# A re-searched instruction order for two transformer layers on one core, with another x tile on ScalarE and an earlier start of the first weight sums

## The chip, the cores and the metric

The kernel runs on one core of a Trainium2 chip. The metric is device microseconds of one execution, the median of three runs. The core has TensorE (PE, the matrix multiplier, with weight loads shown apart as PEld), VectorE (DVE), ScalarE (ACT), GpSimd (POOL) and SyncE (SP), which here issues nearly all DMA transfers. Each engine takes its instructions strictly in the order in which the program lists them, and they wait for each other by semaphores.

## What is computed

Two layers, each made of an attention block A and a feed-forward block B, over x of 2048 rows and 1024 columns:

```python
x = x + A(layernorm(x), wqkv, wo)
x = x + B(layernorm(x), w1, b1, w2, b2)   # and the same pair once more
# A: q, k, v = x @ wqkv; each of 32 heads looks at 8 rows back in steps of 2;
#    softmax over the 8; weighted sum of v; @ wo
# B: h = relu(x @ w1 + b1)**2; h @ w2 + b2      (3584 hidden columns)
```

## The kernel before

The rows are cut into four blocks of 512 rows, and the two layers make eight units (unit 0 to 7), each a block in a layer. A block is four tiles of 128 rows. A unit runs through these stages, named by the functions that write them:

- `SA` loads the four x tiles and normalises them into `xnA`, with features on the partitions. For unit 0 the tiles are loaded in the order 0, 1, 3, 2 (`ORD`). Three of them go through `ln_first`: mean and variance by DVE (`bn_stats`, L791, and their aggregation, L793), the reciprocal root by ACT (L784, L785), the normalisation by DVE (L788). The tile that `LNA` names goes through `ln` instead: ACT makes its statistics by two passes over the tile (L746, L750) with small steps between (L747, L753, L754); if the tile is in `LNV`, DVE normalises it (L759), else ACT does (L756, L725). The normalised tiles of unit 0 are transposed on PE (L807) and copied out by DVE or ACT (L812).
- `SQ` multiplies `xnA` by the q, k and v weights (L888), and ACT writes the results out of PSUM (L893). In unit 0 the first sixteen chunks of k and q are made in halves: first for the tiles 0 and 1, later for 2 and 3. Later units use a seven-product form of block multiplication (`seven`, L663), which needs sums of weights and of inputs. The weight sums are made once and kept in DRAM: `keep_wqkv` (L531), `keep_w1` (L680), `keep_w2` (L457), `keep_wo` (L1108), each a chain of four DVE subtractions and additions with one store each (`sk`, `sqv`, `sw`, `tw`, `two`). The input sums are `TA` (L703) and `T` (L699), on DVE.
- `S2` is the attention: products of q and k on DVE (`P`, L950), their sums (L958), the sum over a head on PE (`lg`, L965), exp on ACT (L976), weighted v on DVE (L1029, L1036).
- `SW` or `SW7` multiplies by wo (L1084, L1155), `SF1` by w1 (L663 again, with L1323 and L1329 on ACT), `SF2` by w2 (L1388), with `yxa` and `yxo` (L1057, ACT) and `xm` (L1058, DVE) behind it.

No engine's order is written out by hand. `Plan` collects every operation with an engine, a planned duration, what it reads and writes, and a priority. `schedule` simulates the engines with these numbers and emits the operations in the order in which they started. `emit` does that several times: the lists in `ORDER` hold seeds, `shift` moves priorities at random by the seeds of the first list, and each later list takes the last schedule's start times as priorities and has `reshift` move some of them. So a list of seeds stands for a whole order of the program, and a change of any seed or of any dependency moves instructions on every engine.

What stands in the code where the change touches it: `ORDER` and the constants above it; in `SA` the branch `u == 0 and tl in LNA`, and the branch `tl == 1`, where `no` is the normalisation (L788) of the second tile; at the end of `SQ` the call of `keep_wqkv` for k in unit 0, whose last argument is a list of operations that the DVE sums (L531) have to follow:

```python
if u == 0 and tl in LNA:
    self.ln(x, xv, [0], xnT, tl, LNP, False, on_pe=True, tag="xn3", after=rst, vnorm=tl in LNV)
...
self.keep_wqkv(nm, ws[nm], [op for op in self.p.ops if op.name == "ptc"] if u == 0 else ())
```

Of the kernel before, what the change touches and what calls it, by code (L numbers as in the profile page):

```python
# [52 lines left out]
RAW = {1: (0, 0), 2: (0, 1), 4: (1, 1)}  # L53
COMB = (5, 7, 6, 3)
RT = 4
LNA = (2,)
LNP = -9e4
LNV = (3,)
AGF = True
FNO = True  # L60
CPA = (1,)
TAIL = True
CPT = ("xn3",)
PR1 = 20.0
# [3 lines left out]
GZ = 6  # L68

ORDER = [  # L70
    [254407839, 254101347, 254903199, 254319407, 254050087, 254927933, 254855223, 254245079, 254581483, 254651541, 254520156, 254414887, 254913701,
    254790479, 254811163, 254451245, 254423391, 254397903, 254011055, 254062271, 254611583, 254031453, 254777341, 254655655, 254059855, 254811767,
    254985755, 254068743, 254312045, 254255164, 254470565, 254340451, 254056147, 254532525, 254814045, 254382679, 254727165, 254873957, 254977849,
    254263075, 254189925, 254540757, 254064125, 254382964, 254486213, 254240707, 254389627, 254830877, 254011075, 254846617, 254426221, 254651009, ],
    [254887702, 254542295, 254553460, 254714252, 254435956, 254354174, 254720528, 254745279, 254184398, 254991686, 254429133, 254634373, 254093956,
    254465069, 254449012, 254670841, 254966233, 254766785, 254298535, 254990048, 254057679, 254666170, 254633564]]

MM = 0.2157
MMH = 0.1091
# [10 lines left out]
def act(n):  # L90
    return 0.05 + n * 0.00084
# [242 lines left out]
class _Kernel:  # L334
# [465 lines left out]
    def transpose(self, xn, xnT, tl, prio, parts=1, act=False):  # L800
# [3 lines left out]
        for i in range(parts):  # L804
# [3 lines left out]

            on_act = act or parts > 1 and i in CPA

# [16 lines left out]
    def SA(self, u):  # L827
        p = self.p
        layer, b = divmod(u, self.NB)
        st = self.state.setdefault(u, {})  # L830
        xnT = Buf("8K", "xnA1" if u == 1 else "xnA", [128, 4, self.KD, 128], F16)
        st["xnA"] = xnT
        after = [self.state[u - 2].get("gatef") or self.state[max(u - 2, 1)].get("gatev")] if u >= 2 else ()
        first, rst = (), []
        for tl in ORD if u == 0 else range(4):
            t = b * 4 + tl
            x, xv = self.load_x(layer, t, after, tag="x0" if u == 0 else "xt", prio=PR1 if u == 1 else -1e6 if u == 0 else None,
                                eng="ACT" if u == 0 and tl in XACT else "SP")
            if u == 0 and tl in LNA:
                self.ln(x, xv, [0], xnT, tl, LNP, False, on_pe=True, tag="xn3", after=rst, vnorm=tl in LNV)  # L840
            elif u == 0:
                bn, ag, r, rest = self.ln_first(x, xv, xnT, tl, first)
                rst.append(r)
                if tl == 0:
                    first, rest0 = [ag] if AGF else [bn], rest
                elif tl == 1:
                    rest0([ag])
                    c, xn, no = rest()
                    first = [no if FNO else c]
                    self.keep_clock(NPB, xn)  # L850
                else:
                    rest()
            else:
                self.ln(x, xv, [0], xnT, tl, PR1 if u == 1 else 20.0, False, vnorm=u in NORM)

    def SQ(self, u, jobs, order=None, halves=()):
        nc, p = self.nc, self.p
        layer, b = divmod(u, self.NB)
        KD, NCH, D = self.KD, self.NCH, self.D
        st = self.state[u]  # L860
        xnT = st["xnA"]
        offs = {"q": 0, "k": HALO, "v": HALO}
        ws = {}
        for nm in jobs:
            self.qkv_buf(u, nm)
            ws[nm] = [Buf("8K", "w", [128, 2, 2, 4, 256], BF) for _ in range(2)]
        pieces = u == 0 and len(jobs) > 1
        for ms in range(4) if pieces else (0, 2):
            for nm in jobs:
                w = ws[nm][ms // 2]  # L870
                if pieces:
                    self.dma(lambda w=w, ms=ms: w[:, ms % 2].rearrange("p a k n -> p (a k n)"), lambda nm=nm, ms=ms: self.wqkv_block(nm, ms), (),
                             [(w, ms % 2)], 0.53, name="w")
                else:
                    self.dma(lambda w=w: w[:].rearrange("p s a k n -> p s (a k n)"),
                             lambda nm=nm, ms=ms: self.wqkv_block(nm, ms, 2).rearrange("(s p) m -> p s m", p=128), (), [(w, 0), (w, 1)], 1.06, name="w")
        if order is None:
            order = [(nm, c0) for nm in jobs for c0 in range(NCH)]

        def chunk(nm, c0, hs, parts=1):  # L880
            pq = Buf("ps", "pq", [128, BLK], F32)
            w, dst, off = ws[nm][c0 // 4], st[nm], offs[nm]
            t0, t1 = hs[0], hs[-1] + 1
            n = KD // parts

            def fm(i):
                for kd in range(i * n, (i + 1) * n):
                    nc.tensor.matmul(pq[:, t0 * HB:t1 * HB], w[:, c0 // 2 % 2, kd // 4, kd % 4, c0 % 2 * 128:c0 % 2 * 128 + 128],  # L888
                                     xnT[:, 2 * t0:2 * t1, kd, :], start=(kd == 0), stop=(kd == KD - 1))
            for i in range(parts):  # L890
                xc = [(xnT, t if i == parts - 1 else (t, i)) for t in range(2 * t0, 2 * t1)]
                st["gate" + nm] = self.pe(4 * len(hs) / parts, lambda i=i: fm(i), xc + [(w, c0 // 2 % 2)], [(pq, h) for h in hs], name="pq")
            p.add("ACT", act(HB * len(hs)), lambda: nc.scalar.copy(dst[:, c0, off + t0 * HB:off + t1 * HB], pq[:, t0 * HB:t1 * HB]),  # L893
                  [(pq, h) for h in hs], [(dst, (c0, h)) for h in hs], 2.0, name="cast")

        for nm, c0 in halves:
            chunk(nm, c0, (0,), 2 if (nm, c0) == halves[0] else 1)
        for nm, c0 in order:
            chunk(nm, c0, (0, 1))
            yield  # L900
        for nm, c0 in halves:
            chunk(nm, c0, (1,))
        for nm in jobs:
            if u == KEEP[nm]:
                self.keep_wqkv(nm, ws[nm], [op for op in self.p.ops if op.name == "ptc"] if u == 0 else ())
            self.halo_out(u, nm)

    def qkv_buf(self, u, nm):
# [450 lines left out]
    def SF2(self, u):  # L1359
# [21 lines left out]
        def mul(name, left, lcells, banks, start, split=False):  # L1381
            for half in range(2):
                w = self.w2_rhs(name, half)
                for q in range(2):
                    def fm(lo=0, hi=BLK, w=w, q=q, half=half):
                        for j in range(g):
                            jj = half * g + j
                            nc.tensor.matmul(banks[q][:, lo:hi], left(jj, q), w[:, j, lo:hi], start=(start and jj == 0), stop=(jj == h - 1),  # L1388
                                             skip_group_check=True)
                    if split and half and q and TAIL:  # L1390
                        xr = xm[3]
# [58 lines left out]
    def out_tile(self, layer, t, db, py, xm, end=False):  # L1450
# [5 lines left out]
        o = lambda: xm[:].bitcast(BF)  # L1456
        if end and TAIL:
            for i in range(2):
# [155 lines left out]
```

## Time and profile before

| | us |
|---|---|
| median of three runs (lowest, highest) | 1137.02 (1135.94, 1138.26) |
| the profiled execution | 1142.31 |
| its span, first to last instruction | 1140.6 |
| PE busy | 1121.8 |
| DVE busy | 995.5 |
| ACT busy | 814.0 |
| PEld busy | 771.2 |
| POOL busy | 1.8 |

PE is busy for 98% of the span. The ends of matmuls are modelled, so its starts say more: warm matmuls that follow each other start 215.7 ns apart with 512 columns and 109.1 ns apart with 256. The mean granted clock of TensorE is 0.999. The DMA engines move 362 MB, 318 GB/s on the mean. The span here is that of the profiled execution, 1.7 us shorter than its own time.

### The profile page before, as it was taken

The page shows a single profiled execution, that of the slowest core. Times are in us where ns is not written, and L with a number is a line of the kernel's source. Part 1 is how long each engine was busy: PE and PEld are TensorE (multiplying, and loading weights), DVE is VectorE, ACT ScalarE, POOL GpSimd, SP SyncE. Part 2 cuts the span into 40 slices and gives each one's busy share as a digit, 9 for nine tenths or more (in the row PEclk, how much of TensorE's full clock was granted, in tenths as well). Part 3 has the DMA queues.
Part 4 walks back from the last instruction along what each step waited for, and adds up shares of the span by engine and source line. Part 5 has one row for each costly group of instructions (what it writes and reads, how often), then busy time and mean ns, then how long its engine had stood idle before and what let it go on. Part 6 is the DMA issues. An engine that isn't in the chain of part 4 may idle for free.

```text
span 1140.6 us, 20659 instructions
## 1 busy us (share of the span) xinstructions
PE 1121.8 (98%) x7857; PEld 771.2 (68%) x7904; DVE 995.5 (87%) x1528; ACT 814.0 (71%) x1628; POOL 1.8 (0%) x8
## 2 busy tenths in 40 slices
PE   8999999998999999999999999999999999999998
PEld 6645864676846787468864688557884678845864
DVE  7999999998997899979999699995999989996341
ACT  7747896566984689757994669847698478943961
POOL 0000000000000000000000000000000000000000
PEclk9999999999999999999999999999999999999999
DMA  9965699999999996999879997899979999589981
GB/s 356 285 217 220 225 317 291 346 343 342 364 339 386 345 377 228 333 396 328 357 281 322 412 335 303 309 310 393 359 271 325 372 354 413 209 304 313 367 299 62
DMA packets 137022, 362.35 MB, mean 318 GB/s; under 512 B 67418, under 2 KB 68570, under 8 KB 116570
## 3 DMA queue, kind: packets, MB, share of 16 engines
q1 hardware_dynamic: 136778, 360.95, 91.3%
q8 instruction: 62, 1.02, 0.4%
q14 instruction: 38, 0.31, 0.1%
q10 hardware_dynamic: 144, 0.07, 0.0%
HBM read 314.84 MB, written 31.46 MB: 304 GB/s over the span
## 4 chain that ended last, share of the span: by engine, by line
PE 64%; ACT 12%; DMA 7%; DVE 2%; issue 1%; SPq 0%; ACTq 0%; DVEq 0%
PE X L663 20%; PE X L1388 12%; PE Z L663 10%; PE Z L1388 6%; PE Y L663 5%; PE X L1155 3%; ACT r L1323 3%; PE Y L1388 3%; ACT rr L1329 2%; PE py L1084 2%; PE Z L1155 1%; DMA w<-in_A_wo_dram 1%; DMA w<-sw 1%; DMA xt<-xs 1%; ACT u L1292 1%
## 5 line engine op out<-in xcount | busy, mean ns | idle before, releaser
L663 PEld LDWEIGHTS <-w 128*128 128x128 f16 (+1 forms) x4904 | 480.4, 98 | 75.9 <-DMA w<-sw 3.0
L1388 PEld LDWEIGHTS <-r 128*128 128x128 f16 x1183 | 115.6, 98 | 136.4 <-issue 3.7
L1388 PE MATMUL X<-w,r 128*128 128x512 f16 (+2 forms) x784 | 177.9, 377 | 1.4 <-ACT yxa L1057 1.0
L950 DVE TENSOR_TENSOR P<-q,k 128x2048 f16<-128x2048 f16 x128 | 154.5, 1225 | 2.2 <-ACT q L626 2.0
L663 PE MATMUL X<-T,w 128*128 128x256 f16 x1224 | 154.0, 273 | 0.1
L1029 DVE TENSOR_TENSOR pr<-pb,v 128x4096 f16<-128x4096 f16 x64 | 146.3, 2297 | 0.4 <-PE Z L663 0.2
L958 DVE TENSOR_TENSOR P<-P,P 128x2048 f16<-128x2048 f16 x110 | 134.2, 1220 | 0.1
L1323 ACT ACTIVATE r<-rr 128x1024 f16<-128x1024 f16 x110 | 123.9, 1139 | 0.3
L1036 DVE TENSOR_TENSOR pr<-pr 128x2048 f16<-128x2048 f16 (+1 forms) x128 | 118.0, 954 | 0.0
L663 PE MATMUL X<-TA,w 128*128 128x256 f16 x864 | 107.6, 273 | 0.0
L596 ACT COPY Y<-X 128x512 f32<-128x512 f32 x115 | 70.2, 610 | 26.0 <-PE X L663 21.5
L888 PE MATMUL pq<-xnA,w 128*128 128x256 f16 (+1 forms) x512 | 86.1, 326 | 2.3 <-DMA w<-in_A_wqkv_dram 0.9
L1302 ACT CAST y<-Z 128x512 f16<-128x512 f32 x110 | 69.5, 646 | 10.5 <-PE Z L663 10.1
L888 PEld LDWEIGHTS <-w 128*128 128x128 bf16 x512 | 49.8, 98 | 34.7 <-issue 1.8
L1306 DVE TENSOR_TENSOR rr<-u,y 128x512 f16<-128x512 f16 x110 | 46.1, 423 | 27.7 <-ACT y L1302 12.8
L663 PE MATMUL X<-xnB,w 128*128 128x256 f16 x440 | 56.9, 277 | 0.0
L1329 ACT ACTIVATE rr<-Y,b1T 128x256 f16<-128x256 f32 x110 | 54.4, 537 | 3.1 <-PE Y L663 2.3
L663 PE MATMUL Y<-xnB,w 128*128 128x256 f16 x440 | 56.4, 273 | 0.0
L663 PE MATMUL Z<-T,w 128*128 128x256 f16 x392 | 51.0, 274 | 4.6 <-DMA w<-sw 2.7
L614 ACT CAST u<-X 128x512 f16<-128x512 f32 x72 | 41.7, 586 | 19.3 <-PE X L663 18.5
L1329 ACT ACTIVATE rr<-X,b1T 128x256 f16<-128x256 f32 x110 | 54.6, 560 | 0.3 <-PE X L663 0.3
L618 ACT CAST yq<-Z 128x512 f16<-128x512 f32 x72 | 41.9, 585 | 16.3 <-PE Z L663 16.3
(168 smaller groups left out, 1653.4 us busy)
## 6 DMA issues: line engine op xcount, KB each, us to landing
w<-sw SPq DMA_DIRECT2D x49, 1024.0 KB, 10.2
w<-tw SPq DMA_DIRECT2D x56, 896.0 KB, 6.6
w<-in_B_w_dram SPq DMA_DIRECT2D x42, 896.0 KB, 6.2
w<-in_B_w_dram SPq DMA_DIRECT2D x35, 1024.0 KB, 10.1
w<-in_A_wqkv_dram SPq DMA_DIRECT2D x32, 1024.0 KB, 10.3
w<-sqv SPq DMA_DIRECT2D x24, 1024.0 KB, 10.9
w<-in_B_w_dram SPq DMA_DIRECT2D x28, 512.0 KB, 5.7
w<-sk SPq DMA_DIRECT2D x12, 1024.0 KB, 7.7
```

Of the source, the lines that this page charges most:

```text
L596: self.p.add("ACT", act(512), lambda: self.nc.scalar.copy(Y[:], X[:]), [(X, 0)], [(Y, 0)], UP, name="u")
L663: nc.tensor.matmul(bank[:, a, :], lw[:, k, a * 128:(a + 1) * 128], rhs(k), start=(start and k == 0 and a == 0), stop=(k == 3), skip_group_ ...
L888: nc.tensor.matmul(pq[:, t0 * HB:t1 * HB], w[:, c0 // 2 % 2, kd // 4, kd % 4, c0 % 2 * 128:c0 % 2 * 128 + 128], xnT[:, 2 * t0:2 * t1, kd, ...
L950: nc.vector.tensor_tensor(cur[:], q[:, c, None, hb * HB:(hb + 1) * HB].to_broadcast([128, W, HB]), _win_ap(k[:, c, :], HALO + hb * HB, HB) ...
L958: nc.vector.tensor_tensor(other[:], other[:], cur[:], ALU.add)
L1029: p.add("DVE", dve(4096), lambda pr=pr, ch=ch: nc.vector.tensor_tensor(pr[:], pb[:].unsqueeze(1).to_broadcast([128, 2, W, HB]), _win_ap2(v ...
L1036: nc.vector.tensor_tensor(dst, pr[:, :, 0:n, :], pr[:, :, n:2 * n, :], ALU.add)
L1302: p.add("ACT", act(512), lambda: nc.scalar.copy(y[:], bank[:]), [(bank, 0)], [(y, 0)], 1.5, name="y")
L1306: p.add("DVE", dve(512), lambda: nc.vector.tensor_tensor(r[:, :, m, :], us[i][:], y[:], ALU.add), [(us[i], 0), (us[i], 1), (y, 0)], [(r, ( ...
L1323: p.add("ACT", 0.955, lambda: nc.scalar.activation(out=r2[:, f:f + 2, :].rearrange("p a t -> p (a t)"), in_=r[:].rearrange("p a m t -> p ( ...
L1329: p.add("ACT", 0.36, lambda a=a: nc.scalar.activation(out=r[:, a, 0, :], in_=bank[:, a, :], func=ACTF.Relu, bias=self.b1T[:, f + a:f + a + ...
L1388: nc.tensor.matmul(banks[q][:, lo:hi], left(jj, q), w[:, j, lo:hi], start=(start and jj == 0), stop=(jj == h - 1), skip_group_check=True)
```

## The change

- `LNA` becomes `(3,)`: the tile with index 3, which is loaded third, has its statistics on ACT. Because 3 is in `LNV`, DVE normalises it (L759) and the ACT steps L756 and L725 of that tile go. The tile with index 2, loaded last, now takes the path by `bn_stats` on DVE.
- `AFTK`: the k sums of unit 0 (`keep_wqkv`, eight DVE operations and eight stores) have to follow only the normalisation of the second tile (`self.opened`), where they had to follow all copies L812 of unit 0 that were planned by then.
- `ORDER` has three lists of other seeds, where it had two. All engines' orders change with it; the counts of instructions stay as they were but for ACT's two that go and DVE's one that comes.

```diff
-LNA = (2,)
+LNA = (3,)
...
+AFTK = True
...
 ORDER = [
-    [254407839, 254101347, 254903199, ...],
-    [254887702, 254542295, 254553460, ...]]
+    [294834927, 294550815, 294025754, ...],
+    [294206791, 294567953, 294362483, ...],
+    [294886139, 294979639, 294680062, ...]]
...
                     first = [no if FNO else c]
+                    self.opened = [no]
...
             if u == KEEP[nm]:
-                self.keep_wqkv(nm, ws[nm], [op for op in self.p.ops if op.name == "ptc"] if u == 0 else ())
+                self.keep_wqkv(nm, ws[nm], () if u else self.opened if AFTK else [op for op in self.p.ops if op.name == "ptc"])
```

The built order of the changed program shows, on each engine, what this comes to where the prediction speaks of it: it names places by the line of the kernel before.

## Prediction

> **What bounds the kernel now.** I read the shares of busy time first, then the waits of PE, the table by stretches, and the timelines of two places where PE stands still. The first line of the page (engine, busy us, share, instructions):
>
> ```profile
> PE 1121.8 (98%) x7857; PEld 771.2 (68%) x7904; DVE 995.5 (87%) x1528; ACT 814.0 (71%) x1628; POOL 1.8 (0%) x8
> ```
>
> PE is the bound, and its work is the same in both kernels. In program order it has 2425 matmuls of 512 columns at 215.7 ns, 5414 of 256 at 109.1 ns and 64 transposes at 56 ns: 523.1 + 590.7 + 3.6 = 1117.3 us. The first matmul starts at 1.11 us, the last ends at 1136.55, and 4.05 us follow. So PE loses 1136.55 - 1.11 - 1117.3 = 18.1 us, and only from these can a new order take anything. Subtracting nominal from traced starts places them: 4.7 in the opening (to 12.5 us), 1.1 at 38, 1.6 at 223, 2.1 at 265, 2.9 at 277 and 1.7 right after, 0.4 at 318, 1.2 at 747, 0.5 at 882, and under 2 in bits. The waits of PE name most (engine, line, waited for: sum, times, longest, us):
>
> ```profile
> PE Z L663 <- DMA w<-sw: 2.7, 1, 2.7
> ...
> PE Z L663 <- DVE T L699: 1.9, 1, 1.9
> ...
> PE py L1084 <- DMA w<-in_A_wo_dram: 1.4, 1, 1.4
> ```
>
> Each happens once. Between 262 and 284 us PE's timeline shows two of them (start, us, operation, [idle before <- releaser]):
>
> ```profile
> 267.50 1.03 PE L663 MATMUL Z<-T,w 128*128 128x256 f16 x8 [1.91 <-DVE T L699]
> ...
> 279.99 1.41 PE L663 MATMUL Z<-T,w 128*128 128x256 f16 x8 [2.74 <-DMA w<-sw]
> 281.19 3.04 PE L663 MATMUL X<-xnB,w 128*128 128x256 f16 x14
> ```
>
> After the second wait 14 matmuls of 256 columns take 3.04 us where 14 x 0.109 = 1.5 are nominal: the granted clock is 0.5 from 280.5 to 283.9 us, which is the 1.7 us. After the 1.91 it stays at 1.
>
> The table by stretches shows what stands close behind PE (stretch, its length, then busy PE, PEld, DVE, ACT, POOL, clock, DMA share, GB/s):
>
> ```profile
> 15.00:60.00 45.00, 44.10 (x326) 31.16 (x324) 42.86 (x47) 33.80 (x81) 0.00 (x0) 1.00 1.07 321
> 60.00:110.00 50.00, 49.89 (x255) 23.93 (x255) 49.80 (x60) 30.59 (x62) 0.00 (x0) 1.00 0.56 199
> 110.00:170.00 60.00, 59.95 (x466) 45.12 (x465) 59.52 (x96) 53.76 (x110) 0.00 (x0) 1.00 0.83 280
> 170.00:225.00 55.00, 53.31 (x296) 29.22 (x300) 52.98 (x69) 33.37 (x65) 0.00 (x0) 1.00 1.03 312
> 225.00:290.00 65.00, 60.30 (x475) 47.07 (x475) 58.95 (x92) 44.25 (x89) 0.00 (x0) 0.97 1.06 352
> ```
>
> Up to 225 us DVE is as full as PE: 205.2 of 210 us from 15 on. Any DVE work added or put later there reaches PE soon. From 215 to 290 us the DMA share is 1.02 to 1.10 in every 15 us.
>
> **Opening.** DVE has its one large gap here:
>
> ```profile
> 9.70 1.91 PE L888 MATMUL pq<-xnA,w 128*128 128x256 f16 x16 [0.48 <-DVE xnA L812]
> ...
> 12.54 1.05 PE L888 MATMUL pq<-xnA,w 128*128 128x256 f16 x8 [0.94 <-DMA w<-in_A_wqkv_dram]
> ...
> 14.07 0.69 DVE L812 COPY xnA<-pt 128x1024 f16<-128x1024 f16 x1 [3.16 <-PE pt L807]
> ```
>
> The k pieces land at 8.66, 9.94 and 11.21 us, the first q piece at 12.49. The new order puts the chunks k0, q0, k1 where they were k0, k1, q0, so one chunk of 8 x 0.109 = 0.87 us now stands behind the landing at 12.49: **+0.9**. ACT's statistics of the third tile (L746 1.24, L747 0.2, L750 1.34 us) stand ahead of or between its xnA copies, which end about 10.7 instead of 9.2; the wait until 12.49 hides that, and without it 1.5 us would be due. The four first k sums (L531, two of 0.65 and two of 0.69 us = 2.67) move into DVE's gap: the third k piece starts them at 11.21, so they end near 13.9, with the normalisations (0.46 and 0.55) about them, and PE asks for those near 14.3. Their stores, 1 MB, now stand ahead of the v weights on SP; v landed at 22.1 and is asked for at about 42, so nothing.
>
> What this gives DVE: 3.16 us of that gap and idle spots of 1.29 and 0.81 us at 25 and 44 make 5.26; off go 1.5 (waiting for the pieces), 0.8 (two casts of q that it takes) and 0.46 (L759). **A lead of about 2.5 us.** The new order spends it. I went through all waits of PE on DVE and set the new place of each operation, in cumulative row durations of its engine, against the old trace. At before's pace DVE would be late by 3.2 us for the first lg (PE's 20th us), by 2.4 to 2.9 at 91 to 160, by 4.4 for TA at 204. Lead plus the 0.9 by which PE itself comes later make 3.4: enough for all but TA, **+1.0** there. Bounds: 0 if the lead is 3.5, +3.5 if it is nothing.
>
> **Transfers, 220 to 290 us.** The second wo load stands one 256-KB store later on SP (about 0.7 us at 350 GB/s), but its producer is 2 us early; it lands near 223.2, and PE, 1.9 later, asks at 224.6: the 1.6 go, so up to here the sum is +0.3. The T wait: the last T stands 2.1 us earlier on DVE's list, and its last input landed at 266.9 and now comes near 262: **-2.1**. The load of sw12 has the same bytes ahead, issued with DVE's lead, so it lands about 277.4 instead of 279.9, and PE asks at 275.3: a wait near 2.1 in place of 2.9 is **-0.8**. It is nearer to the 1.91 that kept the clock than to the 2.74 that lost it, so I take the **-1.7** too. Together -4.3 at 290 us; bounds: if no landing moves, +0.3, since T and wo then come back as a longer wait for sw; if PE stops for none, -6.4.
>
> The Trainium skill ("TensorE: Matmul & The Clock Gate", "Why this matters for your kernels") advises against PE gaps of more than about 3 us and gives an idle window of some 3.4 us as the gate's. Here a wait of 2.74 us lost the clock, so the trace is stricter than the page; the measurement decides. By the page the 1.7 would not hang on this wait, and the sum would be 1.7 higher.
>
> **After 300 us.** ACT waits for x tiles, and PE behind it:
>
> ```profile
> ACT xn L746 <- DMA xt<-xs: 16.2, 4, 6.0
> ...
> PE X L1388 <- ACT yxa L1057: 1.0, 1, 1.0
> ```
>
> The yxa that PE needs stand behind L746 on ACT. The new order puts these L746 4.5 to 9.1 us later, against waits of 3.9 to 6.0: the losses of 1.2 and 0.5 go but for 0.3, **-1.4**. Against that, DVE's operations of units 2, 3 and 6 come up to 3.3, 3.0 and 2.5 us later against PE (places 443, 478, 885). The old trace has 2.85 us of DVE idle at 446 to 481 that would be used up first; **+1.0**, bounds 0 and +8.8. ACT's distances to PE and the end of the program stay. The 1.1 us at 38 stays.
>
> **Sum** on the profiled execution: 0.9 + 1.0 - 1.6 - 2.1 - 0.8 - 1.7 - 1.4 + 1.0 = **-4.7**. But that execution is 1142.31, 5.3 us over the median of 1137.02, with the same work: the timed ones lose less. If the 5.3 are missing from the transfer losses (1.6 + 2.1 + 2.9 + 1.7 = 8.3), those terms shrink from -6.2 by the factor 3/8.3 to -2.2, and the sum is about -0.7; if they are missing elsewhere, it stays -4.7. In the middle, **-2.7: 1134.3 us**.
>
> **Rivals.**
>
> *A: landings don't move.* DMA share is over 1 from 215 to 290 us, the same bytes have to pass, and an earlier issue only queues longer. Then T and wo are paid at sw (+0.3 up to 290 us), and the end gives -1.4 + 1.0: -0.1, 1136.9. For it: the share. Against it: the T that PE waits for hangs on one tile and its place on DVE's list, not on the mean rate. The Trainium skill ("DMA: Bandwidth & Descriptors", "Where 436 GB/s comes from") gives 358 GB/s as the memory's limit for a core; the trace has 402 in 275 to 290 us, so here it doesn't cap the stretch, and by the page this rival would be likelier.
>
> *B: slower, by DVE.* The lead isn't there: the sums in the opening delay the normalisations or the copies behind them in DVE's order. Then PE waits for the first lg and up to TA 4.4 us in all instead of 1.9 (+2.5), and at units 2, 3 and 6 some 6 of the 8.8 (+5.0): -2.7 + 7.5 = +4.8, 1141.8. It decides from a lead of under about 1 us. For it: DVE is 98% busy from 15 to 225 us. Against: the opening gap of 3.16 us is in the trace and the sums fit.
>
> *C: more.* All transfer waits go with the clock, and units 2, 3 and 6 hide their lateness: 1130.5.
>
> That the change doesn't do what it says is excluded by the built order: ACT's first L746 reads the third loaded tile, and the k sums stand ahead of the last copies.
>
> **Chances.** Forecast 0.47 (1131.5 to 1135.5), A 0.22, B 0.22, C 0.09. 0.2%, about what a measurement of this kernel can tell from no change, is 2.3 us. Forecast and C below 1134.7 give 0.45 faster; B beyond 1139.3 and a little of A 0.22 slower; the rest, 0.33, within. The range 1130.5 to 1141 leaves out the far ends of B and C.
>
> **What would show it.** Right: k0 is followed by q0 at about 12.5 us; the first sums at 11.2; no wait for T and for wo, one near 2 us for sw12 at 277 and a granted clock of 1 behind it; PE waiting about 1 us for TA near 206; L746's waits for xs far under 16.2 us in all. Wrong: waits for P, lg or u (DVE) between 20 and 160 us or near 443, 478 and 885 of over 1 us each (B), or sw landing no earlier than 279.9 (A). What I trust least is the lead of 2.5 us and that the new order's small waits elsewhere stay under 1 us each.

## The result and the profile after

The changed kernel takes 1132.91 us (median of 6 runs, 1131.81 to 1134.44) against 1137.51 before (6 runs, 1135.64 to 1138.86): a ratio of 0.9963, 95% interval 0.9951 to 0.9975, 4.2 us less (2.8 to 5.6). 2.7 us less were forecast. The profiled execution of after takes 1133.73 us, 0.8 over its median; that of before, 1142.31, is 4.8 over this median of before (5.3 over the median of three runs that the prediction had).

All waits of PE of 0.3 us or more in the profile after (lines behind the changed places stand 6 or 7 higher: L669 is L663 of before, L895 is L888, L1395 is L1388):

```profile
PE pq L895 <- DMA w<-in_A_wqkv_dram: 1.7, 1, 1.7
PE pk L1517 <- DVE ones L367: 1.1, 1, 1.1
PE pt L813 <- DVE xn L794: 0.9, 1, 0.9
PE pq L895 <- ACT xnA L818: 0.6, 1, 0.6
PE pq L895 <- DVE xnA L818: 0.5, 1, 0.5
PE X L1395 <- ACT X L504: 0.3, 1, 0.3
PE Z L669 <- DMA w<-sqv: 0.3, 1, 0.3
```

The waits for T, sw, wo and yxa are gone, and the first line has grown from 0.9 to 1.7: the five longest all lie in the opening. PE's timeline at the place of the two large waits of before:

```profile
264.86 1.04 PE L669 MATMUL Z<-T,w 128*128 128x256 f16 x8
...
270.49 1.05 PE L669 MATMUL X<-xnB,w 128*128 128x256 f16 x8 [0.23 <-DMA w<-in_B_w_dram]
...
273.99 1.91 PE L669 MATMUL Z<-T,w 128*128 128x256 f16 x16
```

Matmuls follow each other with one gap of 0.23 us, and the clock stays at 1. The table by stretches:

```profile
15.00:60.00 45.00, 45.00 (x341) 32.34 (x339) 43.95 (x45) 35.65 (x85) 0.00 (x0) 1.00 1.09 336
...
225.00:290.00 65.00, 64.47 (x531) 51.64 (x530) 62.51 (x100) 49.87 (x101) 0.00 (x0) 1.00 1.07 374
```

In the last stretch PE is busy for 64.47 of 65 us, against 60.30 before, and 374 GB/s pass instead of 352 at the same DMA share.

**A ledger of PE's lost time.** For each profile below I took each traced start of a matmul minus its nominal place in program order (the reckoning of the prediction), and summed what is lost by stretch. Stretches are cut at nominal places on PE, so that kernels can be compared. Losses in us.

```
                         opening   to wo     wo     218-320  320-585  585-end   sum
before                     4.7      1.4     1.6       7.3      0.5      2.4    17.9
seven others, mean         4.6      0.6     1.5       3.2
              range      4.2-5.2  0.3-2.0  1.1-2.0  2.3-4.7
e2, e4 (after's head)    5.5-5.9  0.3-0.4  0.3-0.5    1.4    0.6-1.1  1.6-1.9  9.8-11.1
e3 (after from 230 us)     5.0      0.9     0.6       1.6      0.5      1.0     9.6
after                      6.1      0.3     0.3       1.1      0.5      1.0     9.4
```

The seven others are the profiles of e1 and e7 to e12 below, which have before's order up to 350 us, three of them with a small edit there. They tell what one profile could not: they lose 2.3 to 4.7 us at 218 to 320, not 7.3. So, by their mean, 4.1 of the 5.3 us by which the profiled execution of before was long (7.3 - 3.2) stood in the waits for T and sw and in the half clock. Against the mean row the change costs 1.5 in the opening and saves 0.3 up to wo, 1.2 at wo and 2.1 at 218 to 320.

The seven are not a fair sample, though. Five of the profiled executions were 1.2 to 3.1 us shorter than the median of their own kernel and two (e9, e10) 0.6 longer, on the mean 1.2 shorter. The granted clock, which is on record for the timed executions beside the experiments too, shows something that they miss. One stretch of 3.41 us at half clock, as in the profile of before, takes 0.0015 off the mean over an execution. Of the 91 executions of before that were timed there, 29 show a mean clock of 0.998, where the profiles without a loss show 0.999 or 1 (0.999 can hold one, as in the profile of before). They take 1138.1 us on the mean, the 43 with a clock of 1 take 1136.9. None of the 20 timed executions of after, e3 and e6 shows 0.998. So about a third of the executions of before, or more, lose the clock somewhere; the timed runs don't tell where.

### The profile page after: what moved, and what is told of

The parts are those of the page before. It is cut to its first block, busy times and chain, and to the rows that moved or that the text cites. A ratio compares the mean times of both kernels' runs of the same rounds, so it can differ in the third digit from the quotient of the medians.

```text
span 1131.7 us, 20621 instructions
## 1 busy us (share of the span) xinstructions
PE 1119.5 (99%) x7858; PEld 770.5 (68%) x7904; DVE 993.7 (88%) x1529; ACT 816.9 (72%) x1626; POOL 1.8 (0%) x8
## 4 chain that ended last, share of the span: by engine, by line
PE 86%; ACT 6%; DVE 3%; DMA 3%; issue 1%; SPq 0%; DVEq 0%; ACTq 0%
PE X L669 22%; PE X L1395 14%; PE Z L669 12%; PE Z L1395 7%; PE pq L895 7%; PE Y L669 6%; PE py L491 4%; PE Y L1395 4%; PE py L1091 3%; PE X L1162 3%; DMA w<-in_B_w_dram 2%; ACT r L1330 1%; PE Z L1162 1%; ACT rr L1336 1%; DVE P L965 1%; PE lg L972 1%
## 5 line engine op out<-in xcount | busy, mean ns | idle before, releaser
L669 PEld LDWEIGHTS <-w 128*128 128x128 f16 (+1 forms) x4904 | 479.6, 98 | 71.0 <-DMA w<-sqv 0.7
L1395 PEld LDWEIGHTS <-r 128*128 128x128 f16 x1183 | 115.8, 98 | 135.0 <-issue 1.7
L1395 PE MATMUL X<-w,r 128*128 128x512 f16 (+2 forms) x784 | 177.2, 377 | 0.6 <-ACT X L504 0.3
L669 PE MATMUL X<-T,w 128*128 128x256 f16 x1224 | 152.6, 273 | 0.0
L669 PE MATMUL X<-TA,w 128*128 128x256 f16 x864 | 107.9, 273 | 0.0
L895 PE MATMUL pq<-xnA,w 128*128 128x256 f16 (+1 forms) x512 | 86.2, 326 | 2.7 <-DMA w<-in_A_wqkv_dram 1.7
L895 PEld LDWEIGHTS <-w 128*128 128x128 bf16 x512 | 49.8, 98 | 34.5 <-DMA w<-in_A_wqkv_dram 2.6
L1336 ACT ACTIVATE rr<-Y,b1T 128x256 f16<-128x256 f32 x110 | 53.7, 526 | 4.7 <-PE Y L669 4.2
L669 PE MATMUL X<-xnB,w 128*128 128x256 f16 x440 | 56.0, 273 | 0.2 <-DMA w<-in_B_w_dram 0.2
L669 PE MATMUL Y<-xnB,w 128*128 128x256 f16 x440 | 56.0, 273 | 0.0
L1064 ACT CAST yxo<-X 128x512 f16<-128x512 f32 x27 | 15.6, 587 | 52.1 <-PE X L1395 52.1
```

The costliest lines, as they stand in the source:

```text
L669: nc.tensor.matmul(bank[:, a, :], lw[:, k, a * 128:(a + 1) * 128], rhs(k), start=(start and k == 0 and a == 0), stop=(k == 3), skip_group_ ...
L1336: p.add("ACT", 0.36, lambda a=a: nc.scalar.activation(out=r[:, a, 0, :], in_=bank[:, a, :], func=ACTF.Relu, bias=self.b1T[:, f + a:f + a + ...
```

## Experiments: where in the order the gain lies

Since the seeds set a whole order, single seeds can't be undone. Instead a kernel gets a list of ranks, one for each operation, which its scheduler reproduces as an order: one kernel's order up to a cut (by planned start), the other's behind it. Ratios are to before, measured in the same rounds; medians beside them can differ from the ratio by 1 us.

```diff
-ORDER = [
...
+RANK = (
...
     def emit(self, place):
...
+        for o, r in zip(self.ops, struct.unpack("<4667H", zlib.decompress(base64.b64decode(RANK)))):
+            o.prio = float(r)
         order, self.timed = self.schedule()
```

**e1, before up to 350 us, then after.** 

> The order of before up to 350 us and the order of after from there on (operations of before). The ledger of PE's lost time in the two profiles gives 2.9 us lost after 350 us in before and 1.5 in after. Theory M (the gain is what the profile shows: the waits at 223 to 284 us go, late losses shrink a little): about 1.4 us under before, 1136.1, with the losses of T and sw still in its profile. Rival L (the waits of the profiled run are mostly absent in the timed runs, so that the timed gain of 4.6 us is made after 350 us): 3 us or more under before, 1134.5 or less.

Measured 1135.54, ratio 0.9984 (0.9975 to 0.9993), 1.8 us less: between both theories and nearer to M. In its profile the T wait was absent and the sw wait 1.5, with the clock kept.

**e2, after up to 350 us, then before.** 

> The order and operations of after up to 350 us and the order of before from there on. Theory M: the rest of the gain, 3 to 3.5 us under before, 1134.0 to 1134.5, with no wait for T or sw in the profile, and the waits of X and Z for yxa near 745 and 880 us back. Rival L: within 1.5 us of before, 1136 to 1137.5.

Measured 1135.45, 0.9985 (0.9975 to 0.9995), 1.7 less. Neither M's 3 to 3.5 nor within L's 1.5: head and tail give about the same, and 1.8 + 1.7 = 3.5 agrees with the whole 4.2 within the intervals. M had taken its size from the one long profile.

**e3, before up to 230 us, then after.** 

> The order of before up to 230 us (its opening, its late k sums, its wait for wo) and the order of after from there on. Theory M (T comes earlier because the last py products, the last sums behind them and so the last input of T stand earlier on PE and DVE, a matter of the order from 230 to 265 us): T and sw waits under 1 us together, 1133.5 to 1134. Rival D (the middle runs on the lead that the early k sums give DVE in the opening; without it DVE is late again and T or sw are waited for): waits of 2 us or more for T, TA or sw in the profile, 1135.5 or more.

Measured 1133.77, 0.9969 (0.9957 to 0.9981), 3.5 less. T and sw are not waited for (0.6 us are lost at 270, where the profile names a weight): M holds. The order from 230 us does without the early sums.

**e4, after up to 230 us, then before.** 

> The order and operations of after up to 230 us (early k sums, third tile on ScalarE, wo) and the order of before from there on. The ledger gives 0.6 to 1.0 us less lost up to 230 us. Theory M: 0.5 to 1 us under before, 1136.5 to 1137, T and sw waited for as in before, together 3 us or more. Rival D: the lead carries the T and sw waits away too, 2.5 us or more under before, 1135 or less.

Measured 1135.21, 0.9985 (0.9976 to 0.9993), 1.7 less, between the two; but its profile is D's: no wait for T or sw although the order from 230 us is that of before. Read so, the sw wait is taken away twice, by the head and by the order behind 230 us, and either is enough. That would explain why the head gives 1.7 us alone (e4), the middle 1.7 alone (e3 less e1), and both no more than 1.7 (e2). It is not shown: the profiled execution of e4 was the shortest of its eleven, and six of the others show a mean clock of 0.998, a loss that this profile doesn't have.

How it is taken away in after shows on SP. First e1 (order of before) with PE's wait, then after; the load of sw that PE waits for is the one behind the pair of stores `two<-tv`:

```profile
259.29 0.57 SPq L422 DMA_DIRECT2D w<-in_B_w_dram  x1
259.91 0.93 SPq L422 DMA_DIRECT2D two<-tv  x2
260.93 0.40 SPq L422 DMA_DIRECT2D w<-sw  x1
...
275.24 1.05 PE L663 MATMUL Z<-T,w 128*128 128x256 f16 x8 [1.50 <-DMA w<-sw]
```

```profile
258.01 0.88 SPq L428 DMA_DIRECT2D two<-tv  x2
259.84 0.32 SPq L428 DMA_DIRECT2D w<-sw  x1
```

In e1 it lands at 275.2, 14.3 us after its issue; in after at 274.4, 14.6 us after. PE would ask at 273.7 in e1 and comes to it at 274.9 in after, as it lost 1.3 us more up to there. So the load was issued 1.1 us earlier and landed 0.8 earlier, and the rest of the wait was paid already: PE lost 1.7 us more in the opening, and made up only part of it at wo. In e4 the load was issued at 261.0, no earlier than in e1, and landed 12.9 us later. So there the wait was absent because the transfer was short and PE came 0.6 us later than in e1. From issue to landing this load took 12.9 to 15.5 us in seven profiles, and nothing here controls that time.

**e11, before up to 600 us, then after.** 

> The order of before up to 600 us and the order of after from there on (operations of before). With the order of after from 350 us the median was 1.9 us under before. Theory X, as for the x tiles (all three places lie behind 590 us): nearly the same, 1.3 to 2 us under before, 1135.3 to 1136. Rival: the gain is made between 350 and 600 us (lg, T and the DVE of units 2 to 4): within 0.6 us of before, 1136.7 to 1137.8.

Measured 1136.20, 0.9987 (0.9975 to 1.0000), 1.5 less: by this nearly all of e1's 1.8 lies behind 600 us, though the interval touches no change.

## Experiments: one part alone

Here single operations move in the emitted order, and all else stays. The numbers in `MOVES` count the operations of the plan; each group goes behind the operation named after it.

```diff
         order, self.timed = self.schedule()
+        for ops, at in MOVES:
+            ops = [self.ops[i] for i in ops]
+            order = [o for o in order if o not in ops]
+            at = order.index(self.ops[at]) + 1
+            order[at:at] = ops
```

**e5, after with the first four k sums late.** `MOVES = (((129, 131, 133, 135, 130, 132, 134, 136), 174),)`: the sums behind the third P and its sum on DVE, their stores behind the v weights on SP. 

> After, with only the first four k sums and their stores put back: on DVE behind the first three P and their sum, on SP behind the v weights. DVE then idles again near 11 to 14 us and has 2.7 us more to do behind it. Theory D (the early sums give DVE the lead on which everything up to 300 us runs): PE waits about 2 to 3 us more for DVE between 20 and 210 us (lg, TA), 1134.5 to 1136, 2 to 3 us over after's 1132.9. Rival S (DVE has that much slack further on; early or late sums make no difference): 1132.5 to 1133.5 and no new wait of over 0.5 us.

Measured 1135.59, 0.9985 (0.9974 to 0.9996), against after's 0.9963: 2.5 us worse. The time is D's, and so is a part of the mechanism. PE waits for the first lg at 30 us:

```profile
28.77 1.22 DVE L965 TENSOR_TENSOR P<-P,P 128x2048 f16<-128x2048 f16 x1
...
30.13 1.02 PE L972 MATMUL lg<-P,grp 128*128 128x512 f16 x4 [1.46 <-ACT sm L759]
```

The profile names a step of ScalarE, but lg reads P, and DVE's sum of P ends at 29.99, just before lg starts. With this wait 1.6 us are lost at the place, and no other wait for DVE is new. The rest is not D's: the wait for the first q weights was 2.03 us in this execution and cost the clock too (below), about 1.3 us. Six of the twelve executions show a mean clock of 0.998 or less; the other six take 1134.3 us on the mean, 1.4 over after's median, which is near the 1.6 of this wait.

**e6, after with k1 ahead of q0 in the opening.** `MOVES = (((69,), 65), ((70,), 66))`. 

> After, with the opening's chunks back in the order k0, k1, q0 on PE and their copies so on ScalarE; all else as in after. The ledger has 4.4 us lost up to the second chunk's end in the order k0, k1, q0 and 5.5 to 6.1 with k0, q0, k1. Theory O (a loss in the opening is a loss at the end): 1 to 1.5 us less, 1131.4 to 1131.9. Rival W (what PE gains in the opening it waits longer for the second wo load near 223 us and for TA near 229, which don't come earlier): opening down by 1 us, those two waits up by as much, 1132.5 to 1133.3.

Measured 1132.47 (6 runs, 1132.01 to 1133.38), 0.9955 (0.9941 to 0.9969): 0.9 us under after by the ratios, which these intervals don't separate. By its time it is at the edge of W's range; its profile speaks for O: the opening loses 5.3 instead of 6.1, and the waits near 223 and 229 did not grow (0.2 in all). This is the fastest version of the study; that it beats after is not shown.

**e7, before with yxa ahead of L746 on ScalarE.** `MOVES = (((2629, 2630), 2570), ((3201, 3202), 3142), ((3774, 3775, 3776, 3777, 3778, 3780), 3715))`; at the third place the tile's later steps on DVE and SP move along. 

> Before, with only ScalarE's order changed at three places near 597, 732 and 867 us: two yxa copies that PE waits for go ahead of the L746 that waits for an x tile from DRAM, as they stand in after. PE's order is that of before. Theory Y (after 350 us the gain is that yxa no longer stands behind L746): 1.2 to 1.9 us less than before, 1135.6 to 1136.3, and no wait of X or Z for yxa near 745 and 882 us. Rival T (it comes from the other moves of the order after 350 us, on DVE and PE): within 0.5 us of before, 1137 to 1138.

Measured 1142.14, 1.0040 (1.0025 to 1.0055): 4.6 us slower. So with before's order on PE this move does not make the gain, and Y falls as far as it rests on the move alone. The top wait of PE in its profile:

```profile
PE X L1388 <- ACT yxa L1057: 4.1, 2, 2.8
```

ScalarE no longer waits for the x tile at those places, but as long for PE's Z, and only then comes the normalisation, now straight ahead of the next pair of yxa (from X), which PE needs too: 1.5 us lost at 744 us and 2.9 at 882. ScalarE's timeline at 738 us:

```profile
738.45 1.07 ACT L1057 CAST yxa<-Z 128x512 f16<-128x512 f32 x2 [6.26 <-PE Z L1388]
739.40 1.07 ACT L746 ACTIVATE xn<-xt 128x1024 f16<-128x1024 bf16 x1
...
743.67 1.05 ACT L1057 CAST yxa<-X 128x512 f16<-128x512 f32 x2
```

**e10, before with x tiles loaded earlier.** `MOVES = (((2628, 2634), 2531), ((3200, 3206), 3103), ((3773, 3779), 3676))`: only SP's order. 

> Before, with only SP's order changed at three places: the loads of the third and fourth x tile (xt from xs) of units 5, 6 and 7 go ahead of the one or two w1 loads that wait for a buffer in front of them, near 588, 724 and 860 us. Theory X (after 350 us the gain is that these x tiles land earlier, so that ScalarE does not stand in L746 with yxa behind it): ScalarE's waits for xs from 16 us to under 8, no wait of X or Z for yxa of over 0.3 us at 745 and 882, 1135.5 to 1136.5. Rival T (other moves of the order after 350 us make the gain; or the w1 loads, now later, are waited for): within 0.5 us of before or slower, 1137 to 1138.5.

Measured 1136.79, 0.9988 (0.9976 to 1.0001), 1.4 less. ScalarE's waits for these tiles, 16.2 us in four times before:

```profile
ACT xn L746 <- DMA xt<-xs: 1.9, 1, 1.9
```

The same waits are 8.4 to 16.5 us in all six profiles with before's order there, so this part of X is shown. No wait for yxa is left, and 0.8 us are lost from 585 to the end, against 2.4 in before and 1.0 in all six profiles with after's order there. But e8 and e12, with before's order there, lose 0.8 too and have no wait for yxa, so this one profile can't show what the earlier loads save. The time agrees with X, but its interval just reaches 1.

**e8, before with the first four k sums early.** `MOVES = (((129, 131, 133, 135), 29),)`: only DVE's order. 

> Before, with only the first four k sums moved on DVE, from behind the first three P into the gap at 11 to 14 us, behind the third tile's normalisation; their stores, and everything on PE, ScalarE and SP, as in before. Theory D (the early sums alone give the lead, and the lead takes away waits at 223 to 280 us): 1.5 to 2.5 us less, 1135 to 1136, the waits for wo and sw together 1.5 us shorter. Rival P (PE's own order at 230 to 290 us is what matters, and DVE's lead is used up or waits elsewhere): within 0.7 us of before, 1136.8 to 1138, wo and sw waited for as before.

Measured 1138.05, 1.0008 (0.9993 to 1.0022): nothing gained. Rival P's result, and DVE's timeline tells why: the gap of 3.16 us is filled, and opens again behind it.

```profile
13.85 0.69 DVE L812 COPY xnA<-pt 128x1024 f16<-128x1024 f16 x1 [0.20 <-PE pt L807]
20.68 1.23 DVE L950 TENSOR_TENSOR P<-q,k 128x2048 f16<-128x2048 f16 x1 [1.43 <-ACT q L893]
25.43 0.69 DVE L1496 TENSOR_TENSOR b2d<-b2b 128x512 f32<-128x512 bf16 x1 [2.25 <-DMA b2b<-in_B_b_dram]
```

**e12, as e8, and b2d behind the next four operations.** `MOVES = (((129, 131, 133, 135), 29), ((168,), 183))`. 

> As the run with the early k sums in before's order, which left the time as it was, because DVE then idled 1.43 us for q (at 20.7 us) and 2.25 us for the bias of b2d (at 25.4 us); here b2d (one DVE operation) also goes behind the next four operations, as it stands in after. Theory L (the lead was lost at b2d): the 2.25 us go to under 0.7, DVE keeps 1.5 us, and the waits for wo, T and sw are together 1 us or more shorter than in the run without it: 1135.5 to 1136.7. Rival N (the next operations aren't ready either, or the lead is lost again up to 225 us): 1137 to 1138.5, DVE idle elsewhere in 15 to 60 us.

Measured 1137.32, 1.0001 (0.9990 to 1.0013). Rival N: the idle time moves on.

```profile
21.11 1.23 DVE L950 TENSOR_TENSOR P<-q,k 128x2048 f16<-128x2048 f16 x1 [1.47 <-ACT q L893]
41.51 1.23 DVE L950 TENSOR_TENSOR P<-q,k 128x2048 f16<-128x2048 f16 x1 [1.12 <-PE lg L965]
43.81 0.18 DVE L926 COPY halo<-k 128x56 f16<-128x56 f16 x1 [1.06 <-ACT k L893]
```

The lead of DVE can be read as the DVE time done in the first 60 us (third column after the length). Before, e8, e12 and after, in this order:

```profile
0.00:60.00 60.00, 55.41 (x401) 37.91 (x402) 50.88 (x69) 42.22 (x101) 1.75 (x8) 1.00 1.02 319
```

```profile
0.00:60.00 60.00, 56.70 (x407) 38.61 (x408) 52.17 (x69) 42.95 (x102) 1.76 (x8) 1.00 1.02 330
```

```profile
0.00:60.00 60.00, 56.84 (x402) 38.34 (x403) 51.79 (x69) 42.41 (x102) 1.76 (x8) 1.00 1.03 335
```

```profile
0.00:60.00 60.00, 55.08 (x399) 37.76 (x400) 53.69 (x70) 42.80 (x103) 1.76 (x8) 1.00 1.03 330
```

In all, the profiles with after's head and early sums (after, e2, e4, e6) have 53.7 to 54.3; those with before's head 50.8 to 52.0, and with the sums alone (e8, e12) 52.2 and 51.8. The rest of after's head without the early sums makes none either (e5: 50.8). The sums make a lead only together with the rest of after's order in the first 60 us.

**e9, before with the last wo sum early.** `MOVES = (((1038,), 1104),)`: only DVE's order. 

> Before, with one DVE operation moved: the last sum of wo (L1108), which stands at 265.6 us, goes ahead of a T, a P product and a second P product to 262 us; its store stands on SP ahead of the sw load that PE waits for at 275 us. Theory H (that load is held on SP behind the store): it is issued 2 us or more earlier, the wait for sw (1.5 to 1.9 us in the three profiles of this order that kept the clock) goes to under 0.5, 1135.3 to 1136.3. Rival Q (the load's time is set by its buffer or by the transfers ahead of it): it is still issued near 266.8 us and lands 8 us later, the wait stays over 1.2 us, within 0.7 us of before.

Measured 1136.96, 0.9998 (0.9989 to 1.0007). The experiment took the wrong store: the load of sw that PE waits for stands ahead of this store, behind those of the second and third sum, as the lines of e1 above show. It was issued at 261.5 us, no earlier than in e1, and landed at 277.1; the sw wait was only 0.6 because PE waited 2.0 for T just before. So theory H fails for this store. For the stores of the second and third sum it was not tried.

What the third tile's statistics on ScalarE are worth alone was not tried either.

## Why the prediction was right, step by step

The sign, the range and the main place (218 to 320 us) were right; the size was 2.7 us for a measured 4.2, just under the lower end of its interval, 2.8 to 5.6. The terms fit less well than the total.

- **Opening, +0.9.** 6.1 lost in after, 4.6 in the mean of before's order: +1.5. Right in kind, too small; the q weights landed about half a microsecond later than in the profile of before.
- **A lead of 2.5 us.** DVE has done 54.0 us of work by 60 us in the mean of after's head and 51.4 in that of before's order (e8 and e12 left out): 2.6. The size was right. That it would come from filling the gap was half the story: e8 fills the gap and gets nothing.
- **TA, +1.0 for DVE.** Not so: 0.4 lost at 229 us, and what the profile names there is a transfer (w from sqv, 0.26). DVE was on time.
- **wo, -1.6.** 0.3 left in after. Right.
- **T, -2.1.** Gone, but it was worth less: in six of the seven other profiles of before's order 0 to 0.9 us were lost at this place, and only in e9 2.15.
- **sw, -0.8, with 2.1 left.** Here the step failed: nothing is left. It had PE ask at 275.3 and the load land at 277.4. PE came at 274.9, so the first was right; the load landed at 274.4, 3.0 us before the forecast. That had been reckoned from the one long execution, in which the load was issued at 264.88 and took 15.1 us; in e1, with the same order, it was issued at 260.93 and took 14.3.
- **Clock, -1.7.** Right for the profiled execution, but not a term of every one. Among the seven others only e10 lost the clock there, and about a third of the timed executions of before lost it somewhere, while none of after's six shows 0.998: as an estimate from these, a third of 1.7, some 0.6 us on the mean.
- **After 300 us, -1.4.** 2.4 became 1.0 from 585 us on, but the mean of six profiles with before's order there is 1.7 (0.8 to 2.5), so the size is -0.7. The prediction put it down to L746 standing later on ScalarE. e7 makes that move in before's order, and is slower; e10 lets the x tiles land earlier, and ScalarE's waits go. In after more moves at once: at 733 us PE also delivers the first Z for yxa earlier (yxa starts at 732.9 and 734.7; in e7, which runs 2.5 us later here, both from 738.5). Which of these makes the gain is not shown.
- **DVE at units 2, 3 and 6, +1.0.** Nothing: 0.5 lost at 320 to 585 in both, and the small new waits of PE at 451 and 988 us (0.21 and 0.26) are for copies on ScalarE.
- **The 5.3 us.** The prediction halved between "in the transfer losses" and "elsewhere". By the mean of the seven, 4.1 of them were in the transfer losses. By that branch alone the sum was -0.7; most of what it misses are the costs that did not come (TA 0.6, units 2, 3 and 6 1.0) and the sw wait that went whole (1.5 to 2.2 lost there in six of the seven others, where the scaled term took 0.3). That the middle of the two branches came near the measured time is in part luck: too much was taken off for waits of one long execution and too much added for costs that did not come.

Rival A (landings don't move) is half borne out: from issue to landing the sw load takes about as long in after (14.6 us) as in e1 (14.3). But it was issued earlier, and A's end did not follow. The Trainium skill ("DMA: Bandwidth & Descriptors", "Where 436 GB/s comes from") would have capped the stretch at 358 GB/s; the profile after has 415 from 270 to 290 us, so the trace disagrees, and goes with the 425 for one core alone that the same page lists under "Bandwidth". Rival B did not occur. Rival C, at 0.09, is what the profile after looks like: the waits for T, wo and sw gone, the clock kept, no lateness at units 2, 3 and 6. Its 1130.5, for which the prediction shows no sum, was not reached.

The ledger's terms, +1.5 - 0.3 - 1.2 - 2.1 and -0.7 (mean 1.7 from 585 us on in the six profiles with an unedited order of before there, 1.0 in after), make -2.8. The remaining 1.4 to the measured 4.2 us are as much as its interval. Most or all of them can be the choice of executions: the seven profiled ones were 1.2 us shorter than their kernels' medians, and after's was 0.8 longer. In which waits these 2.0 us lie is not shown; losses of the clock are likely some of them.

## What to carry over

Before a wait in one profile is priced, look whether the profiled execution is as long as the timed ones: here most of 5.3 us too much sat in two waits and a clock loss that seven other profiles of the same order have, on the mean, at half the size. One profile for each order is no sample either: those seven were 1.2 us shorter than their kernels' medians. An early operation gives an engine a lead only if what stands behind it in the engine's order is ready early as well; otherwise the idle time moves a few operations on, as in e8 and e12. And where an engine stands in a wait with something needed behind it, bring what it waits for earlier (e10) before reordering around it (e7).

## What the runs showed of the hardware

The clock of TensorE falls after a shorter stop than expected, but the length of the stop alone does not decide. Idle PE time before the wait's end, and the granted clock behind it (last column but two): 1.83 us in e7 and 1.91 in before kept it; 1.99 in e9 kept it; 2.00 in e10, 2.03 in e5 and 2.74 in before lost it; and a second wait of e7, 2.76 us at 882 us, kept it. First e9, then e10, then e5, then e7:

```profile
266.70 1.03 PE L663 MATMUL Z<-T,w 128*128 128x256 f16 x8 [1.99 <-DVE T L699]
...
266.70:268.00 1.30, 1.30 (x12) 1.17 (x13) 1.30 (x4) 0.23 (x1) 0.00 (x0) 1.00 1.00 422
```

```profile
276.76 1.85 PE L663 MATMUL Z<-T,w 128*128 128x256 f16 x8 [2.00 <-DMA w<-sw]
...
278.00:280.00 2.00, 2.00 (x11) 1.45 (x10) 1.54 (x2) 0.96 (x2) 0.00 (x0) 0.50 1.05 429
```

```profile
13.21 3.21 PE L895 MATMUL pq<-xnA,w 128*128 128x256 f16 x16 [2.03 <-DMA w<-in_A_wqkv_dram]
...
13.20:15.00 1.80, 1.79 (x9) 1.27 (x10) 0.00 (x0) 0.00 (x0) 0.00 (x0) 0.50 1.03 414
```

```profile
882.81 6.20 PE L1388 MATMUL X<-w,r 128*128 128x512 f16 x28 [2.76 <-ACT yxa L1057]
...
884.00:886.00 2.00, 2.00 (x11) 0.88 (x9) 1.96 (x3) 0.39 (x3) 0.00 (x0) 1.00 1.00 410
```

The traces hold the times at which the clock changes, and these fall on a fixed grid: from one change to the next it is a whole number of steps of 3.413 us (one step at half clock in before, e5 and e10; at full clock 2 in e5, 80 in e10, 81 in before, 332 in e7). Where the grid lies differs from execution to execution: its first change is at 3.8 us in e10 and at 6.9 in e9. I summed PE's lost time within each step, as in the ledger. In the 14 profiles, up to the last matmul, the clock is halved behind the three steps at full clock in which most was lost (2.16 us in e10, 2.55 in e5, 2.88 in before), and behind none in which less was (the largest 1.99, in e7). The 2.76 us of e7 (2.93 by the ledger's reckoning) lie across a border at 881.6 us, 1.7 lost before it and 1.2 behind. So here the clock is lost when PE loses some 2.0 to 2.2 us or more within one step, and whether a wait of 2 to 3 us costs it is a matter of where the step's border falls. That is inferred from these traces; no run shifted the grid on purpose.

Losing the clock costs 1.3 to 1.7 us more, nearly the wait again. The Trainium skill ("TensorE: Matmul & The Clock Gate", "Why this matters for your kernels") warns of gaps over about 3 us; here three shorter ones, 2.00, 2.03 and 2.74 us, lost the clock, and the measurement decides.
